# Holding the weight conversions behind block 0's activations, a reciprocal spread by matrix products, and one store per weight chunk

## The chip, the cores and the metric

The kernel runs on one core of a Trainium2 chip. The metric is device time in microseconds (us). Three runs of the kernel before gave 976.02, 977.13 and 977.84 us; their median is 977.13.

## The reference

Three layers follow each other. All inputs are float32, except that the eight-byte weights `w_in` and `w_out` arrive as pairs of 32-bit words, which the kernel has to convert to float32 itself.

1. Linear attention, 8 batches, 8 heads, 576 positions, 64 features: `phi(x)` projects by `w_phi` (64 to 128), subtracts the largest absolute value of the row, and joins `exp(p)` with `exp(-p)`. With `k_p = phi(k)` and `q_p = phi(q)`: `kv = k_p' v`, `z = sum(k_p)`, and the output is `(q_p kv) / (q_p z + 1e-6)`.
2. A dense layer over the 4608 tokens with 512 features: `h = x w_in` (2048 wide), a leaky rectifier with a slope `alpha` for each of the 2048 columns, and a product with `w_out`.
3. A soft mixture of 8 experts with 4 slots each: logits from `phi`, a softmax over all tokens, a two-layer network in each expert, and a softmax over slots for the way back.

## The kernel before

The 4608 tokens are cut into 12 blocks of 384 (`NB`, `BT`); `w_in` is cut into 16 chunks of 128 columns (`NC`). One slot of the program is one product of a block with a chunk: `gemm(n, c)` (L531), 12 matmuls of 128x384 with `x` and `w_in` each split in a high and a low part (`xhi`, `xlo`, `w` in the wring pool). Block n fills slots 16n to 16n+15. Slots below 0 are the opening, in which there is no `gemm` yet. `at(slot, phase, fn)` puts all other work in a slot, before the product ("pre"), beside it ("pe", "pe2") or behind it ("post"). A planner then orders the instructions of each engine ahead of time: it goes by a simulated time line and takes, among the instructions that are ready, the one that stands first in the program. So the order on an engine is fixed when the kernel starts, and an instruction that waits holds up all that stand behind it on its engine. All loads and stores go through one queue, that of SP, in order. A `nosync` dependency between two instructions of one engine fixes only their order in this plan.

The work around the change:

- `conv` (L185) converts a chunk, or two at once, of `w_in` or `w_out`. It loads the words into `raw` (three buffers, L190 to L192), takes the absolute value on ScalarE (ACT, L200) and runs six operations on VectorE (DVE, L201 and L205 to L212). `use_w_in` splits the result: the high part on ACT (L226), the low part on DVE (L227). `behind` (L202) orders the first operations behind others; before, chunks 0 to 2 name key features there, chunk 3 and the pairs from 4 on name nothing. Chunks 0 to 3 sit at slots -30, -26, -22 and -3, the pairs from chunk 4 on at slots 0, 2, 4, ... 10.
- `use_w_out` stores each converted chunk of `w_out` to DRAM in four pieces (L235), and multiplies it with `phi` on TensorE (PE) for the logits. The `w_out` pairs begin at slot 10.
- `k_pair` (L263) makes keys and values of two heads: `project` (L297), `features` (L283: a reduction L285, a subtraction L287, two exponentials L290 and L291), `kv` (L340 to L348), `turn` and `keep` (L362, L369). Pairs 0 to 3 serve batch 0 and so block 0, pairs 4 to 7 batch 1; block 1 needs both. The projected keys lie in the PSUM tile `banks("pk")`, which has one buffer and is shared with the query projections of blocks from 1 on.
- `q_pair` (L389) projects queries, takes the largest absolute value over partitions on GpSimd (POOL, L423), and in `attend` makes `num` and `den` (L444, L449).
- `q_finish` (L461) turns these into `x`: a reciprocal of `den` (L466, L467), a spread of it over partitions, a multiplication, and the split into `xhi` (ACT, L484) and `xlo` (DVE, L485). Block 0 spreads by 16 small matmuls with columns of the identity (`spread`, L488, results in PSUM, L495 multiplies). All other blocks store the reciprocal to DRAM (L470), load it back with every row repeated (`widen`, L475), and multiply (L502). Block 0 divides 1 slot after its reciprocal, block 1 3 slots, the others 6. `xhi` and `xlo` have one buffer each, so block 1's `x` is written only when block 0's last product has read its own.
- `leaky` (L543) takes each product out of PSUM with ACT (L545) and DVE (L546); two PSUM buffers stand for it.

Of the kernel before, what the change touches and what calls it, by code (L numbers as in the profile page):

```python
# [11 lines left out]
I32 = mybir.dt.int32  # L12
U32 = mybir.dt.uint32
AF = mybir.ActivationFunctionType
ALU = mybir.AluOpType
AX = mybir.AxisListType
# [10 lines left out]
BT = 384  # L27
# [34 lines left out]
def attention_prelu_softmoe(ctx: ExitStack, tc, qT, kT, v, wphi, w_in, w_out, alpha, phi, w1, w2, out):  # L62
    nc = tc.nc

    ps_h = ctx.enter_context(tc.tile_pool(name="ps_h", bufs=2, space=PSUM))
# [47 lines left out]
    def bank(name, pool=None):  # L113
        if pool is not None:
            return pool.tile([128, 512], F32, tag={id(ps_h): "h", id(ps_l): "l", id(ps_d): "d"}[id(pool)], name=name)
        taken["a"].append([])
        return ps_a.tile([128, 512], F32, tag="a", name=name)
# [67 lines left out]
    def conv(slot, srcs, uses, behind=None):  # L185
        st = {}
        n = len(srcs)

        def load():
            st["raw"] = prep.tile([128, 2, 1024], I32, tag="raw", name="raw", bufs=3)[:, 0:n]  # L190
            for j in range(n):
                nc.sync.dma_start(st["raw"][:, j], srcs[j])  # L192

        def first():
            pair = st["raw"].rearrange("p c (n t) -> p c n t", t=2)
            st["low"], high = pair[:, :, :, 0].bitcast(U32), pair[:, :, :, 1]
            m = st["m"] = prep.tile([128, 2, 512], F32, tag="m", name="m", bufs=2)[:, 0:n]
            rest = st["rest"] = high.bitcast(F32)
            mu, ru = m.bitcast(U32), rest.bitcast(U32)
            heads = [nc.scalar.activation(m, high.bitcast(F32), AF.Abs)]  # L200
            heads.append(nc.vector.tensor_scalar(out=m, in0=m, scalar1=F64_LEAST, scalar2=F64_MOST, op0=ALU.max, op1=ALU.min))  # L201
            if behind is not None:  # L202
                for ins, other in zip(heads, done_k[behind]):
                    tc.add_manual_dep(ins.ins, other.name, nosync, reason="behind the features of K")
            nc.vector.tensor_scalar(out=mu, in0=mu, scalar1=3, scalar2=0x3FFFFFFF, op0=ALU.logical_shift_left, op1=ALU.bitwise_and)  # L205
            nc.vector.scalar_tensor_tensor(out=mu, in0=high.bitcast(U32), scalar=0xC0000000, in1=mu, op0=ALU.bitwise_and, op1=ALU.bitwise_or)  # L206
            nc.vector.tensor_scalar(out=ru, in0=mu, scalar1=0xFF800000, scalar2=None, op0=ALU.bitwise_and)
            nc.vector.scalar_tensor_tensor(out=rest, in0=st["low"], scalar=2.0 ** -52, in1=rest, op0=ALU.mult, op1=ALU.mult)  # L208

        def second():  # L210
            m = st["m"]
            mark[slot + 1] = nc.vector.tensor_tensor(out=m, in0=m, in1=st["rest"], op=ALU.add).ins  # L212
            for j, use in enumerate(uses):
                use(slot + j, m[:, j])

        at(slot - 2, "pre", load)
        at(slot, "pre", first)
        at(slot + 1, "pre", second)
# [12 lines left out]
    def use_w_out(c):  # L231
        def use(slot, w):
            st = {}
            for i in range(4):
                nc.sync.dma_start(wo32[4 * i + c // 4, 32 * (c % 4):32 * (c % 4) + 32, :], w[32 * i:32 * i + 32])  # L235

            def trans():
                pt = bank("pwt")
                for k in range(KD):
                    nc.tensor.transpose(pt[:, 128 * k:128 * k + 128], w[:, 128 * k:128 * k + 128], ident)  # L240
                st["wT"] = prep.tile([128, 512], F32, tag="wT", name="wT")
                nc.scalar.copy(st["wT"], pt)

            def product():
                pw = bank("pw", ps_l)
                for k in range(KD):
                    nc.tensor.matmul(pw[32 * k:32 * k + 32, 0:128], phi_sb[:, k, :], st["wT"][:, 128 * k:128 * k + 128], start=True, stop=True)
                st["sw"] = prep.tile([128, 128], F32, tag="sw", name="sw")
                nc.scalar.copy(st["sw"], pw[:, 0:128])

            def gather():
                pw = bank("pw2", ps_l)
                nc.tensor.matmul(pw[:, 0:32], st["sw"], tident[:, 0:32], start=True, stop=True)
                nc.vector.tensor_copy(wpr[:, c, :], pw[:, 0:32])

            at(slot + 2, "pe", trans)
            at(slot + 3, "pe", product)
            at(slot + 4, "pe", gather)
        return use
# [3 lines left out]
    def k_pair(slot, i):  # L263
# [18 lines left out]

        def features(src, dst, nt, read):  # L283
            mx = att.tile([128, 4], F32, tag="mx", name="mx", bufs=4)
            nc.vector.tensor_reduce(out=mx[:, 0:nt], in_=src, axis=AX.X, op=ALU.max, apply_absolute_value=True)  # L285
            neg = dst[:, :, 1, :]
            ins = nc.vector.tensor_tensor(out=neg, in0=src, in1=mx[:, 0:nt].unsqueeze(2).to_broadcast([128, nt, F]), op=ALU.subtract).ins  # L287
            if read is not None:
                read.append(ins)
            nc.scalar.activation(dst[:, :, 0, :], neg, AF.Exp)  # L290
            done_k[i] = nc.scalar.activation(neg, neg, AF.Exp, scale=-1.0).ins, ins  # L291
# [169 lines left out]
    def q_finish(slot, n):  # L461
        st = q_st[n]

        def recip():
            rd = sm.tile([128, BT], F32, tag="dT", name="rd")[:, 0:HB]
            nc.vector.tensor_scalar(out=rd, in0=st["den"][:, 0:HB], scalar1=1e-6, scalar2=None, op0=ALU.add)  # L466
            nc.vector.reciprocal(out=rd, in_=rd)  # L467
            st["rd"] = rd
            for j in range(2 if n else 0):
                nc.sync.dma_start(rc_d[n % 2][j].rearrange("p h t -> h p t"), rd[64 * j:64 * j + 64])  # L470

        def widen():
            bc = st["bc"] = xp.tile([128, NP, BT], F32, tag="bc", name="bc")
            for j in range(2):
                nc.sync.dma_start(  # L475
                    bc[64 * j:64 * j + 64], rc_d[n % 2][j, 0:NP].rearrange("p h t -> p (h t)").unsqueeze(0).to_broadcast([64, NP, BT]))

        def scale(p):
            def go():
                if p == 0:  # L480
                    xhi_t[n] = xp.tile([128, KD, BT], F32R, tag="xhi", name="xhi")
                    xlo_t[n] = xp.tile([128, KD, BT], F32R, tag="xlo", name="xlo")
                xs = st["num"][:, p, :]
                nc.scalar.copy(xhi_t[n][:, p, :], xs)  # L484
                nc.vector.tensor_tensor(out=xlo_t[n][:, p, :], in0=xs, in1=xhi_t[n][:, p, :], op=ALU.subtract)  # L485
            return go

        def spread(p):  # L488
            wide = bank("wide", ps_h)
            together([  # L490
                lambda j=j, h=h, sl=slice(64 * j, 64 * j + 64): nc.tensor.matmul(
                    wide[sl, HB * h:HB * h + HB], ident[sl, 64 * j + 32 * h + p:64 * j + 32 * h + p + 1].to_broadcast([64, 64]), st["rd"][sl],
                    start=True, stop=True)
                for h in range(2) for j in (1, 0)])
            nc.vector.tensor_tensor(out=st["num"][:, p, :], in0=wide[:, 0:BT], in1=st["num"][:, p, :], op=ALU.mult)  # L495

        def divide(p):
            def go():
                if n == 0:
                    return spread(p)  # L500
                xs = st["num"][:, p, :]
                ins = nc.vector.tensor_tensor(out=xs, in0=st["bc"][:, p, :], in1=xs, op=ALU.mult).ins  # L502
                tc.add_manual_dep(ins, mark[max(k for k in mark if k <= slot + wait)].name, nosync, reason="behind the load")
            return go

        wait = (1, 3)[n] if n < 2 else 6
        at(slot, "post", recip)
        if n:
            at(slot + 1, "pre", widen)
        for p in range(NP):  # L510
            at(slot + wait, "post", divide(p))
        for p in range(NP):
            at(slot + wait, "post", scale(p))
# [175 lines left out]
    for n in range(NB):  # L689
# [3 lines left out]
            else:  # L693
                q_pair(NC * (n - 1) + 3 * p - 6 - (p > 0) if n > 2 else 12 + 2 * p if n > 1 else (0, 2, 5, 8)[p], n, p)
        q_finish((-22, 12)[n] if n < 2 else NC * (n - 1) + 7, n)
    for c, slot, behind in ((0, -30, 2), (1, -26, 3), (2, -22, 3), (3, -3, None)):
        conv(slot, [w_in[c].bitcast(I32)], [use_w_in], behind)
    for c in range(4, NC, 2):
        conv(c - 4, [w_in[d].bitcast(I32) for d in (c, c + 1)], [use_w_in] * 2)
    for c in range(0, NC, 2):  # L700
        conv(int(10 + 1.2 * c), [w_out[d].bitcast(I32) for d in (c, c + 1)], [use_w_out(d) for d in (c, c + 1)])
    for n in range(NDEF, NB):
# [286 lines left out]
```

## Time and profile before

| what | value |
|---|---|
| three runs, median (lowest to highest) | 977.13 us (976.02 to 977.84) |
| the profiled execution's own time | 975.91 us |
| its span, first to last instruction | 973.9 us |
| its mean granted TensorE clock | 0.987 |
| PE busy with matmuls | 931.4 us, 96% of the span |
| PE weight loads (PEld), which run beside matmuls | 653.7 us, 67% |
| DVE busy | 709.7 us, 73% |
| ACT busy | 410.3 us, 42% |
| POOL busy | 148.4 us, 15% |

Times inside the profile count from the first instruction, and the profiled execution's own time is 2.0 us longer than its span. A busy share is an average over the whole span, in which the opening (the first 70 us) and the later blocks are very different. The granted clock is 1.00 at the full level of 2.4 GHz and 0.50 at 1.2 GHz; a mean between them is a stretch that holds both.

### The profile page before, as it was taken

The numbers are of one execution on the slowest core, as the hardware profiler recorded it, in microseconds if no ns is written. First come the engines' busy times: TensorE is split into PE (matmuls) and PEld (weight loads), VectorE is DVE, ScalarE is ACT, GpSimd is POOL, SyncE is SP. The second block draws the span as 40 slices with busy tenths as digits, with TensorE's granted clock in tenths as the row PEclk, the third lists the DMA queues.
The fourth block names the chain that finished last, engine by engine and source line by source line (L and its number), as shares of the span: only waits on it lengthen the run. The fifth ranks groups of instructions, "written<-read, shape, count | busy, mean of one in ns | idle before, by whom it ended". The sixth has DMA issues, their size and how long they took to land.

```text
span 973.9 us, 19896 instructions
## 1 busy us (share of the span) xinstructions
PE 931.4 (96%) x8210; PEld 653.7 (67%) x8210; DVE 709.7 (73%) x1341; ACT 410.3 (42%) x789; POOL 148.4 (15%) x84
## 2 busy tenths in 40 slices
PE   7978996999999999999999999999999999899997
PEld 4546774677767676676677676776777767787444
DVE  6899996897577587767777677777766767865233
ACT  6655654545445334345345336354343351221113
POOL 5111220301201212122021122111021220000000
PEclk9979998999999999999999999999999999999999
DMA  7346665553131131021121121210111508588999
GB/s 262 116 162 206 204 207 154 176 173 114 54 87 34 31 84 44 23 78 44 35 71 42 33 72 31 70 31 23 46 34 51 178 29 269 172 270 265 329 351 327
DMA packets 75382, 121.34 MB, mean 125 GB/s; under 512 B 7836, under 2 KB 49308, under 8 KB 75292
## 3 DMA queue, kind: packets, MB, share of 16 engines
q1 hardware_dynamic: 75292, 120.07, 39.5%
q8 instruction: 65, 1.06, 0.5%
q14 instruction: 25, 0.20, 0.1%
HBM read 99.03 MB, written 21.00 MB: 123 GB/s over the span
## 4 chain that ended last, share of the span: by engine, by line
PE 79%; DVE 13%; ACT 4%; DMA 2%; issue 1%; SPq 0%; ACTq 0%; DVEq 0%
PE ph L538 39%; PE num L444 6%; PE pkv L340 5%; PE pS L643 4%; PE pl L574 4%; PE den L449 3%; PE pq L411 3%; PE pk L297 2%; PE pso L887 2%; PE pe L867 1%; PE po L923 1%; DVE m L206 1%; DVE m L212 1%; PE pt L362 1%; DVE raw L208 1%
## 5 line engine op out<-in xcount | busy, mean ns | idle before, releaser
L538 PE MATMUL ph<-xhi,w 128*128 128x384 f32 x1536 | 433.4, 351 | 11.5 <-ACT xhi L484 6.1
L538 PEld LDWEIGHTS ph<-xhi,w 128*128 128x128 f32 x1536 | 279.4, 189 | 74.6 <-issue 41.0
L538 PE MATMUL ph<-xlo,w 128*128 128x384 f32 x768 | 257.3, 341 | 0.1
L423 POOL PARTITION_ALL_REDUCE mb<-pj x48 | 141.9, 2957 | 468.4 <-ACT pj L417 374.2
L545 ACT ACTIVATE gT<-ph 128x384 f32<-128x384 f32 x192 | 93.7, 489 | 252.6 <-PE ph L538 248.5
L546 DVE SCALAR_TENSOR_TENSOR gT<-gT,alpha_rest,ph 128x384 f32<-128x384 f32 x192 | 115.7, 603 | 109.2 <-ACT gT L545 108.4
L538 PEld LDWEIGHTS ph<-xlo,w 128*128 128x128 f32 x768 | 144.3, 189 | 11.4 <-issue 8.0
L565 DVE STREAM_TRANSPOSE gb<-gT 128x384 f32<-128x384 f32 x162 | 91.8, 571 | 3.0 <-issue 0.2
L433 ACT ACTIVATE qe<-pj 128x768 f32<-128x768 f32 x90 | 71.8, 838 | 26.7 <-DVE pj L427 18.3
L444 PE MATMUL num<-qe,kv 128*64 128x192 f32 (+1 forms) x488 | 70.0, 412 | 3.6 <-ACT kall L290 2.3
L340 PE MATMUL pkv<-kall 128*64 128x256 f32 x464 | 57.5, 391 | 2.9 <-ACT num L454 1.8
L285 DVE TENSOR_REDUCE mx<-pk 128x4 f32<-128x512 f32 (+1 forms) x80 | 49.5, 623 | 10.4 <-PE pk L297 9.1
L290 ACT ACTIVATE kall<-kall 128x512 f32<-128x512 f32 x60 | 37.5, 627 | 37.6 <-DVE kall L287 37.4
L411 PE MATMUL pq<-qraw,wp 64*128 64x384 f32 x192 | 46.6, 544 | 6.5 <-DMA qraw<-in_qT_dram 3.8
L444 PEld LDWEIGHTS num<-qe,kv 128*64 128x64 f32 x488 | 31.2, 136 | 27.8 <-issue 17.9
L328 DVE TENSOR_TENSOR ks<-ks,kall 128x256 f32<-128x256 f32 x96 | 47.5, 511 | 0.4
L340 PEld LDWEIGHTS pkv<-kall 128*64 128x64 f32 x464 | 31.2, 138 | 23.9 <-issue 5.8
L427 DVE TENSOR_TENSOR pj<-pj,mb 128x768 f32<-128x768 f32 x48 | 44.7, 932 | 2.4 <-POOL mb L423 2.4
L449 PE MATMUL den<-qe,zt 128*32 128x192 f32 x720 | 42.0, 337 | 1.7 <-ACT qe L433 1.7
L287 DVE TENSOR_TENSOR kall<-pk,mx 128x512 f32<-128x512 f32 x60 | 40.9, 681 | 2.4 <-PE pkv L340 1.7
L454 ACT COPY num<-num 128x384 f32<-128x384 f32 x48 | 22.7, 476 | 44.2 <-PE num L444 42.5
L297 PE MATMUL pk<-wp,kall 64*128 64x128 f32 x512 | 38.9, 290 | 2.3 <-DMA kall<-in_kT_dram 1.3
(204 smaller groups left out, 1104.5 us busy)
## 6 DMA issues: line engine op xcount, KB each, us to landing
w<-in_w_dram SPq DMA_DIRECT2D x46, 256.0 KB
kall<-in_v_dram SPq DMA_DIRECT2D x30, 320.0 KB
qraw<-in_qT_dram SPq DMA_DIRECT2D x48, 192.0 KB
out_dram<-os SPq DMA_DIRECT2D x18, 512.0 KB
bc<-rc_d SPq DMA_DIRECT2D x22, 384.0 KB
raw<-in_w_in_dram SPq DMA_DIRECT2D x16, 512.0 KB
raw<-in_w_out_dram SPq DMA_DIRECT2D x16, 512.0 KB
gT_d<-gT SPq DMA_DIRECT2D x32, 192.0 KB
```

Source lines behind the costliest of these rows:

```text
L285: nc.vector.tensor_reduce(out=mx[:, 0:nt], in_=src, axis=AX.X, op=ALU.max, apply_absolute_value=True)
L297: lambda t=t, j=j, sl=slice(64 * j, 64 * j + 64): nc.tensor.matmul(st["pk"][:, j, F * t:F * t + F], st["kraw"][sl, 128 * t:128 * t + 128], ...
L340: return lambda: nc.tensor.matmul(pkv[64 * j:64 * j + 64, 0:256], st["vt"][:, t, 64 * j:64 * j + 64], part.rearrange("p s f -> p (s f)"), ...
L411: lambda j=j, sl=slice(64 * j, 64 * j + 64): nc.tensor.matmul(pq[j][:, 0:BT], wp[sl, F * j:F * j + F], st["qraw"][sl], start=True, stop=True)
L423: nc.gpsimd.partition_all_reduce(mb, pj, 128, bass_isa.ReduceOp.absmax)
L433: nc.scalar.activation(st["e", s], pj, AF.Exp, scale=(1.0, -1.0)[s])
L444: lambda s=s, j=j: nc.tensor.matmul(num[64 * j:64 * j + 64, o:o + w], kvs[:, s, 64 * j:64 * j + 64], st["e", s][:, j, o:o + w], start=(s = ...
L449: lambda s=s, j=j, h=h, zt=kv_t[NP * ((n * BT + h * HB) // S) + p][1]: nc.tensor.matmul(den[64 * j + 32 * h:64 * j + 32 * h + 32, 0:HB], z ...
L538: gemm_last[0] = nc.tensor.matmul(h, (w_in_hi, w_in_lo)[a][c][:, 128 * k:128 * k + 128], (xhi, xlo)[b][:, k, :], start=(i == 0), stop=(i = ...
L545: nc.scalar.activation(gT, h, AF.Relu, scale=-1.0)
L546: ins = nc.vector.scalar_tensor_tensor(out=gT, in0=gT, scalar=alpha_rest[:, c:c + 1], in1=h, op0=ALU.mult, op1=ALU.add).ins
L565: nc.vector.transpose(out=half_of(n, c // 8)[:, c % 8, :], in_=gT)
```

## The change

Three edits, in one step.

1. Chunks 2 and 3 of `w_in` move to slots -19 and -16, and all conversions of `w_in` from chunk 2 on are ordered behind block 0's `x`: their first ACT operation behind the last `xhi` copy, their first DVE operation behind the last `xlo` subtraction (both now kept in `done_k["x", n]`). The feature reductions of key pairs 4 and 5 are ordered behind that `xlo` too.
2. Block 1's reciprocal is spread by 16 matmuls, as block 0's is, into PSUM tiles of the pool that most of the attention uses (`bank(...)` with no pool, two buffers). Its two stores to DRAM, its two loads back and its tile `bc` are gone, and its division stands 1 slot after the reciprocal instead of 3.
3. `use_w_out` stores a chunk with one DMA of 128 rows instead of four of 32.

```diff
-            for i in range(4):
-                nc.sync.dma_start(wo32[4 * i + c // 4, 32 * (c % 4):32 * (c % 4) + 32, :], w[32 * i:32 * i + 32])
+            nc.sync.dma_start(wo32[c // 4::4, 32 * (c % 4):32 * (c % 4) + 32, :], w)
...
-            nc.vector.tensor_reduce(out=mx[:, 0:nt], in_=src, axis=AX.X, op=ALU.max, apply_absolute_value=True)
+            ins = nc.vector.tensor_reduce(out=mx[:, 0:nt], in_=src, axis=AX.X, op=ALU.max, apply_absolute_value=True).ins
+            if 4 <= i < 6:
+                tc.add_manual_dep(ins, done_k["x", 0][1].name, nosync, reason="behind block 0's x")
...
-            for j in range(2 if n else 0):
+            for j in range(2 if n > 1 else 0):
...
-                nc.scalar.copy(xhi_t[n][:, p, :], xs)
-                nc.vector.tensor_tensor(out=xlo_t[n][:, p, :], in0=xs, in1=xhi_t[n][:, p, :], op=ALU.subtract)
+                done_k["x", n] = (
+                    nc.scalar.copy(xhi_t[n][:, p, :], xs).ins,
+                    nc.vector.tensor_tensor(out=xlo_t[n][:, p, :], in0=xs, in1=xhi_t[n][:, p, :], op=ALU.subtract).ins)
...
         def spread(p):
-            wide = bank("wide", ps_h)
+            wide = bank("wide", None if n else ps_h)
+            read = taken["a"][-1:] if n else []
...
-            nc.vector.tensor_tensor(out=st["num"][:, p, :], in0=wide[:, 0:BT], in1=st["num"][:, p, :], op=ALU.mult)
+            ins = nc.vector.tensor_tensor(out=st["num"][:, p, :], in0=wide[:, 0:BT], in1=st["num"][:, p, :], op=ALU.mult).ins
+            for r in read:
+                r.append(ins)
...
-                if n == 0:
+                if n < 2:
                     return spread(p)
...
-        wait = (1, 3)[n] if n < 2 else 6
+        wait = 1 if n < 2 else 6
...
-        if n:
+        if n > 1:
             at(slot + 1, "pre", widen)
...
-    for c, slot, behind in ((0, -30, 2), (1, -26, 3), (2, -22, 3), (3, -3, None)):
+    for c, slot, behind in ((0, -30, 2), (1, -26, 3), (2, -19, ("x", 0)), (3, -16, ("x", 0))):
...
-        conv(c - 4, [w_in[d].bitcast(I32) for d in (c, c + 1)], [use_w_in] * 2)
+        conv(c - 4, [w_in[d].bitcast(I32) for d in (c, c + 1)], [use_w_in] * 2, ("x", 0))
```

## Rows read from the trace of the kernel before

**Rows 1.** The page: busy time and share of the span, instructions, per engine.

```profile
PE 931.4 (96%) x8210; PEld 653.7 (67%) x8210; DVE 709.7 (73%) x1341; ACT 410.3 (42%) x789; POOL 148.4 (15%) x84
```

**Rows 2.** Six stretches: length, busy time of each engine, granted clock, DMA share.

```profile
0.00:37.00 37.00, 30.88 (x337) 18.32 (x339) 23.33 (x55) 24.18 (x44) 12.65 (x16) 1.00 0.60 198
37.00:71.60 34.60, 27.84 (x267) 16.05 (x264) 34.46 (x59) 19.13 (x33) 4.51 (x2) 0.85 0.46 167
71.60:137.10 65.50, 59.42 (x535) 46.89 (x535) 64.46 (x86) 33.99 (x58) 14.95 (x8) 0.97 0.60 198
137.10:170.00 32.90, 23.92 (x192) 16.85 (x191) 25.29 (x44) 17.13 (x34) 3.88 (x3) 0.90 0.57 172
170.00:190.00 20.00, 19.36 (x156) 12.94 (x155) 19.45 (x28) 9.53 (x17) 7.65 (x3) 1.00 0.53 168
190.00:250.00 60.00, 58.93 (x458) 46.53 (x457) 49.57 (x94) 31.13 (x62) 8.69 (x4) 1.00 0.49 143
```

**Rows 3.** Time line of PE, 39 to 67 us: end of block 0's attention, spread, first product.

```profile
39.37 1.43 PE L348 MATMUL pkv<-kp,ones 128*32 128x128 f32 x40
42.37 0.55 PE L362 MATMUL pt<-ident,kvT 128*128 128x128 f32 x3
47.66 0.51 PE L449 MATMUL den<-kall,zt 128*32 128x192 f32 x8
55.96 2.83 PE L491 MATMUL wide<-rd,ident 64*64 64x192 f32 x16 [2.30 <-DVE rd L467]
61.68 1.52 PE L491 MATMUL wide<-rd,ident 64*64 64x192 f32 x16
66.55 0.97 PE L538 MATMUL ph<-xhi,w 128*128 128x384 f32 x4
```

**Rows 4.** Time line of DVE, 42 to 72 us: a conversion's operation, the keep, the reciprocal, `x`.

```profile
42.70 0.68 DVE L212 TENSOR_TENSOR m<-m,raw 128x512 f32<-128x512 f32 x1
43.30 0.42 DVE L207 TENSOR_SCALAR raw<-m 128x512 uint32<-128x512 uint32 x1
44.96 0.42 DVE L369 COPY kv<-pt 128x256 f32<-128x256 f32 x1
51.90 0.35 DVE L466 TENSOR_SCALAR rd<-den 128x192 f32<-128x192 f32 x1
54.57 1.34 DVE L467 RECIPROCAL rd<-rd 128x192 f32<-128x192 f32 x1
59.03 0.54 DVE L495 TENSOR_TENSOR num<-wide,num 128x384 f32<-128x384 f32 x1
71.04 0.55 DVE L485 TENSOR_TENSOR xlo<-num,xhi 128x384 fp32r<-128x384 f32 x1
```

**Rows 5.** Block 1's reciprocal: time lines of DVE, SP's queue and PE, 134 to 156 us.

```profile
135.78 1.35 DVE L467 RECIPROCAL rd<-rd 128x192 f32<-128x192 f32 x1
134.98 5.23 SPq L235 DMA_DIRECT2D wo<-m  x8
141.76 1.19 SPq L470 DMA_DIRECT2D rc_d<-rd  x2
147.04 1.47 SPq L475 DMA_DIRECT2D bc<-rc_d  x2
153.83 0.56 DVE L502 TENSOR_TENSOR num<-bc,num 128x384 f32<-128x384 f32 x1 [6.90 <-DMA bc<-rc_d]
140.17 0.34 PE L538 MATMUL ph<-xhi,w 128*128 128x384 f32 x1
154.99 1.33 PE L538 MATMUL ph<-xhi,w 128*128 128x384 f32 x3 [6.05 <-ACT xhi L484]
```

**Rows 6.** Stretches of 4 us, columns as in rows 2: the clock after both stalls.

```profile
52.00:56.00 4.00, 1.70 (x10) 0.52 (x6) 4.00 (x7) 2.19 (x3) 0.00 (x0) 0.50 0.74 282
152.00:156.00 4.00, 1.01 (x3) 0.82 (x3) 2.17 (x5) 1.57 (x3) 0.00 (x0) 0.71 0.50 164
156.00:160.00 4.00, 4.00 (x19) 2.28 (x18) 4.00 (x9) 1.56 (x4) 0.00 (x0) 0.50 0.28 82
```

**Rows 7.** SP's queue, whole span: one line's issues, least/median/most ns, first and last.

```profile
L235 SPq DMA_DIRECT2D wo<-m x64: 302/423/1200, 127.5 to 239.8; - x64
```

**Rows 8.** The page, DMA issues: tiles, count, size of one issue.

```profile
bc<-rc_d SPq DMA_DIRECT2D x22, 384.0 KB
raw<-in_w_in_dram SPq DMA_DIRECT2D x16, 512.0 KB
```

## The prediction

> **What bounds the kernel now.** I read the page's busy times first. PE is busy 96% of the span [rows 1], so the whole can only lose what PE idles or does at half clock. Then I cut the first 250 us into stretches, since the edits touch nothing behind them [rows 2]. Idle PE is length minus busy: 6.1 us to 37, 6.8 in 37.0 to 71.6, 6.1 in 71.6 to 137.1, 9.0 in 137.1 to 170, 0.6 to 190, 1.1 to 250. Beside it stands DVE: 34.46 of 34.6 and 64.46 of 65.5 us, so from 37 to 137 DVE has no free time, and whatever PE lacks there it lacks because DVE has not yet come to it. In 137.1 to 170 it is the other way: DVE is busy 25.29 of 32.9 us, and both engines wait.
>
> The time lines say for what. First stall: block 0's last attention product ends at 48.2 [rows 3], but its reciprocal begins at 51.9, ends at 55.9, and the last `xlo` ends at 71.6 [rows 4], since each of these steps stands in DVE's order among conversions and key features. PE idles or runs at the 1.2 GHz level meanwhile (clock 0.50 in 52 to 56 with 1.70 of 4 us busy [rows 6]). Second stall: block 1's reciprocal ends at 137.1; SP is then issuing eight stores of `w_out` (134.98, 5.23 us), so the reciprocal's stores go at 141.8, the loads back at 147.0, and the first multiplication runs at 153.8, after DVE has idled 6.90 us. Block 0's last product ended at 140.5, block 1's first starts at 155.0 after 6.05 us of idle PE [rows 5], and the clock is then 0.50 to 160 [rows 6].
>
> **Part by part.** The sum is made against the profiled execution's own 975.9 us; the median of the runs shown is 1.2 us above that.
>
> *The reciprocal of block 1.* Removed: two stores, two loads, and the wait for them. Added: 16 products of 64x192, which block 0's show at 1.52 us at full clock and 2.83 us at half [rows 3]. The four multiplications read PSUM instead of SBUF: 0.54 us against 0.56 [rows 4, 5], so nothing. What can be won is the slack of 137.1 to 170 [rows 2]. On PE: 9.0 us idle, and the half clock, which cost half of the 4.00 us busy in 156 to 160 and half of the 1.01 in 152 to 156 [rows 6], 2.5 together; less 1.5 for the added products, 10.0 us. On DVE the same stretch can shrink only by its idle 32.9 - 25.3 = 7.6 us. Which of the two rules is not shown by the stretch itself: from 170 to 190 PE is busy 19.36 and DVE 19.45 of 20 us, but from 190 to 250 DVE has 10.4 us to spare and PE 1.1 [rows 2], so a DVE that is late can be made good and a PE that is late cannot. I take the middle, 8.8, and keep 7.6 and 10.0. What is late next: `xhi` has one buffer, so block 1's `x` waits for the end of block 0's last product. With the spread, the reciprocal no longer ends last there; that product does, and PE has the key products and `w_out` transposes in between to fill the half microsecond of the copies.
>
> *The hold behind block 0's `x`.* It removes no work; it reorders DVE and ACT. Without conversions in the way, the chain is this. The counts of key pair 3 end at 40.8 and the turn at 42.9 [rows 3]; the keep now starts at once instead of at 44.96 [rows 4], so the 2.0 us it waited go, and `den` ends at 46.1 instead of 48.2. The reciprocal takes 0.35 + 1.34 = 1.7 us: 47.8. Half a microsecond for the first spread product and its latency (an estimate: a quarter of the 1.52 us of all 16): 48.3. Then four multiplications and four subtractions at 0.54 and 0.55 [rows 4], 4.4 us: `x` is whole at 52.7 instead of 71.6, 18.9 us sooner.
>
> But DVE pays for it. Between 37 and 52.7 it may now do only the rest of chunk 1 (five operations of at most 0.68 us, 3.4), two keeps (0.8), the reciprocal (1.7) and `x` (4.4): 10.3 of 15.7 us [rows 4]. The other 5.4 us it idles, where it had 0.1 us idle in the whole stretch [rows 2]. What was done there before is done after 52.7, so DVE reaches its old state of 71.6 about 5.4 us late. Chunks 0 and 1 are enough for PE's first two products, but the third needs chunk 2, and the third needs also that `leaky` of the first has been run, behind the held work in DVE's order. With no slack on DVE until 137 [rows 2], the 5.4 us reappear whole at block 1's reciprocal: 137.1 becomes about 142.5, and block 0's last product ends near 146 instead of 140.5. Block 1's first product then follows within a microsecond or so of it, at 146 to 148 instead of 155.0. The bill is 5.4; its bounds are nothing (if work that DVE does early now need not be done before block 1) and 10.7 (5.4 and one wait for a load, see the last rival). Below nothing is excluded: an order alone cannot make DVE's work less. The half clock of the first stall gives nothing back by itself, since DVE paces that part.
>
> *Behind the hold* stand on ACT the absolute values of the chunks, on DVE the features of key pairs 4 and 5, and through their PSUM tile the first query projections of block 1 on PE. All of these serve block 1, 80 us away, and cost nothing beyond the bill. On SP the load of pair 6/7 now waits for chunk 2's buffer; all later loads queue behind it. About 15 us of held DVE work cover that wait.
>
> *One store for four.* 48 issues of 0.42 us [rows 7] leave SP's queue between 127 and 240. The case where that was in the way, the 5.23 us ahead of the reciprocal's stores [rows 5], is gone through the spread already. What is left is at most the 1.7 us that PE idles from 170 to 250 [rows 2]; the buffer is freed by the last of the four stores as by the one, so it costs nothing. I take nothing.
>
> Sum: -8.8 + 5.4 = -3.4. 975.9 becomes 972.5, and a median of runs 1.2 above it: **973.7 us**.
>
> The Trainium skill speaks against counting PE here: its page "Perfetto Trace Analysis", section "Identifying the Most-Contended Engine", holds that matmul busy time is a poor measure of how near a kernel is to its limit, that weight-load share should be used for TensorE, and that for VectorE the busy share is a fair measure. In 71.6 to 137.1 the weight loads fill 46.89 of 65.5 us beside 59.42 for matmuls and 64.46 for DVE [rows 2], so the trace agrees for that stretch. By that rule DVE's time alone would count, to 190 at least, which is the first rival.
>
> **The rivals.**
>
> 1. DVE alone decides, no change. Only DVE's own idle time counts: 7.6 us won in 137.1 to 170, against 5.4 lost in the hold, or 6.6 if neighbouring operations overlap by 0.08 us as 42.70 + 0.68 against a start at 43.30 shows [rows 4] (15 operations). Net -1.0 to -2.2, so about 975.5. For it: DVE's busy time up to 190 [rows 2]. Against: its 10.4 us of slack right after. Chance 0.19.
> 2. The hold is free. If the planner puts other work into the 5.4 us, or what DVE did early was not needed before block 1, the full PE side counts: -10.0, and -1.7 with the stores: 965.4. For it: PE idles 6.8 us in the first stall. Against: DVE is busy without a break for 100 us. Chance 0.13.
> 3. The spread blocks PE. The products stand in PE's order and wait there for the reciprocal, as block 0's did for 2.30 us [rows 3], and share two PSUM buffers with all the attention. The change would then not do all it says: -3.4 + 2.3, 976.0. Chance 0.06.
> 4. Slower: the conversions starve. Chunks 2 and 3 now hold two of three `raw` buffers through the hold, and SP's queue stands still behind the load of pair 6/7. If the held work does not cover it, DVE waits a whole load: 384 KB took from 148.5 to 153.8, 5.3 us [rows 5], and the pair is two of 512 KB [rows 8]. Then -7.6 + 5.4 + 5.3 = +3.1, 980.2. It decides from the point where DVE waits over 4 us for words between 53 and 100. For it: the deep prefetch is what let DVE run without a break. Against: the 15 us of cover. Chance 0.17.
>
> **How the numbers follow.** My forecast has 0.45, with its own range of 970.5 to 975.1. About 0.2%, 2 us, is what a measurement here can tell from no change. Faster by more: forecast and rival 2, 0.58. Within it: rivals 1 and 3, 0.25. Slower: rival 4, 0.17. The range of 8 in 10 reaches to both far cases, 966.5 to 980.5, and leaves out about half of rival 2 and half of rival 4.
>
> **What would show it.** Hold: the last `xlo` of block 0 near 53, and DVE idle of some 5 us between 37 and 53; if DVE idles under 2 us, rival 2. Bill: block 1's reciprocal ending near 142.5; at 137 or sooner the bill was wrong. Spread: no DVE idle over 2 us around it, no `ph` wait of 6 us, block 1's first product at 146 to 148, clock 1.00 from 150 to 160. Rival 3 would show as a PE wait on `wide` for `rd`. Rival 4 as DVE or ACT idle before L200 and L201 between 53 and 100. The forecast is wrong altogether if PE's idle time after 170 grows by more than it shrank before.

## The result and the profile after

The changed kernel takes 982.75 us (median of 4 runs, 980.80 to 984.18) against 976.58 us for the kernel before in the same session: a ratio of 1.0062 with a 95% interval of 1.0038 to 1.0086. By that ratio it is slower by 6.1 us, where 3.4 us less were forecast. The profiled execution took 982.11 us, its span is 980.2 us. Lines have moved by a few: `spread` is now L494, its multiplication L498, `xhi` L486, `xlo` L487, `gemm` L543, the store L234.

The busy times of the page, to lay beside [rows 1], hardly differ, so the change lies in where the engines wait:

```profile
PE 936.7 (96%) x8242; PEld 656.5 (67%) x8242; DVE 704.4 (72%) x1341; ACT 409.5 (42%) x789; POOL 152.1 (16%) x84
```

The stretches of [rows 2] from 37 us on, same columns:

```profile
37.00:71.60 34.60, 28.50 (x294) 19.41 (x290) 27.66 (x52) 15.25 (x28) 5.89 (x2) 1.00 0.42 146
71.60:137.10 65.50, 58.46 (x527) 42.85 (x528) 65.47 (x90) 40.78 (x69) 20.61 (x10) 0.97 0.56 192
137.10:170.00 32.90, 22.74 (x149) 16.07 (x148) 26.64 (x42) 9.67 (x20) 1.69 (x1) 0.74 0.46 149
170.00:190.00 20.00, 20.00 (x160) 13.55 (x160) 15.55 (x25) 11.52 (x21) 6.45 (x3) 1.00 0.65 207
190.00:250.00 60.00, 58.50 (x473) 46.14 (x468) 50.36 (x90) 32.40 (x63) 7.67 (x5) 1.00 0.46 138
```

In the first two the hold does what it says: DVE is idle for 6.9 of 34.6 us and then without a break, and the clock of the first stall is 1.00 instead of 0.85. The third got worse, though the spread was to empty it: PE is busy 22.74 us instead of 23.92, at a clock of 0.74 instead of 0.90.

The time line of DVE, to lay beside [rows 4] and [rows 5]:

```profile
45.69 0.36 DVE L467 TENSOR_SCALAR rd<-den 128x192 f32<-128x192 f32 x1 [3.05 <-PE den L450]
52.75 1.03 DVE L487 TENSOR_TENSOR xlo<-num,xhi 128x384 fp32r<-128x384 f32 x2
...
135.62 1.34 DVE L468 RECIPROCAL rd<-rd 128x192 f32<-128x192 f32 x1
...
144.18 1.21 DVE L212 TENSOR_TENSOR m<-m,raw 128x1024 f32<-128x1024 f32 x1
...
149.52 0.56 DVE L498 TENSOR_TENSOR num<-wide,num 128x384 f32<-128x384 f32 x1
156.29 0.69 DVE L201 TENSOR_SCALAR m<-m 128x1024 f32<-128x1024 f32 x1 [6.22 <-ACT m L200]
```

Block 0's `x` is whole at 53.8 us (71.6 before). Block 1's reciprocal ends at 137.0, as before. But the first `w_out` pair is converted (L212) only at 145.4, and after one multiplication of block 1 DVE stands still for 6.22 us. PE and ACT in the same place:

```profile
145.44 1.97 PE L239 MATMUL pwt<-ident,m 128*128 128x128 f32 x8 [6.24 <-DVE m L212]
147.34 0.66 PE L246 MATMUL pw<-wT,phi_sb 128*32 128x128 f32 x8
147.92 1.55 PE L494 MATMUL wide<-rd,ident 64*64 64x192 f32 x8
149.40 0.64 PE L252 MATMUL pw<-tident,sw 128*128 128x32 f32 x2
149.96 2.83 PE L494 MATMUL wide<-rd,ident 64*64 64x192 f32 x16
156.71 1.33 PE L543 MATMUL ph<-xhi,w 128*128 128x384 f32 x3 [3.92 <-ACT xhi L486]
```

```profile
155.14 1.12 ACT L200 ACTIVATE m<-raw 128x1024 f32<-128x1024 f32 x1 [6.33 <-DMA wo<-m]
156.16 0.50 ACT L486 CAST xhi<-num 128x384 fp32r<-128x384 f32 x1
```

Two stalls have taken the place of the one of 6.05 us in [rows 5]. PE first waits 6.24 us for the late `w_out` pair, whose transposes stand in its order ahead of the spread. Then ACT, whose next instruction is the absolute value of the third `w_out` pair, waits 6.33 us for a store of `w_out` to free that pair's buffer; `xhi` of block 1 stands behind it, so PE waits another 3.92 us. The clock answers as in [rows 6]:

```profile
152.00:156.00 4.00, 0.79 (x6) 0.17 (x2) 0.00 (x0) 0.86 (x1) 0.00 (x0) 0.50 0.50 156
156.00:160.00 4.00, 3.29 (x17) 1.94 (x19) 3.71 (x7) 1.18 (x3) 0.00 (x0) 0.50 0.60 240
```

SP issued that store at 145.41:

```profile
145.41 1.27 SPq L234 DMA_DIRECT2D wo<-m  x2
146.73 1.48 SPq L192 DMA_DIRECT2D raw<-in_w_out_dram  x2
```

It is two stores of 256 KB, one for each chunk of the pair. The last of the two issues ended at 146.68, and ACT went on at 155.14: 8.5 us. The DMA view of 145.4 to 157 us in 40 slices (busy share of the 16 DMA engines in tenths, and what they moved) shows how:

```profile
DMA  0000131495689999999433322232222496799999
GB/s 0 0 0 0 42 35 7 21 113 85 127 304 346 388 396 353 388 381 403 177 155 155 127 106 78 92 92 71 71 85 106 127 226 198 282 388 388 410 374 396
```

While a load of `raw` runs beside it, the share is 8 or 9 tenths for most of the time and 300 to 400 GB/s move. When that load is nearly through, the share falls to 2 or 3 tenths, what 4 busy engines of 16 would give, and the rate to 71 to 155 GB/s. The single packets in the trace say the same: the pair's 256 packets of 2 KB run from 146.7 to 154.7 us, mostly 4 at a time.

### The profile page after: what moved, and what is told of

It is laid out like the page before. It is cut to its first block, busy times and chain, and to the rows that moved or that the text cites. A ratio compares the mean times of both kernels' runs of the same rounds, so it can differ in the third digit from the quotient of the medians.

```text
span 980.2 us, 19895 instructions
## 1 busy us (share of the span) xinstructions
PE 936.7 (96%) x8242; PEld 656.5 (67%) x8242; DVE 704.4 (72%) x1341; ACT 409.5 (42%) x789; POOL 152.1 (16%) x84
## 4 chain that ended last, share of the span: by engine, by line
PE 83%; DVE 8%; DMA 4%; ACT 3%; issue 1%; SPq 0%; DVEq 0%; ACTq 0%
PE ph L543 39%; PE pkv L341 7%; PE num L445 7%; PE pS L648 4%; PE pl L579 4%; PE den L450 4%; PE pq L412 3%; PE pk L298 3%; PE pso L892 2%; PE pe L872 1%; PE po L928 1%; PE pt L363 1%; DVE gT L551 1%; DMA wo<-m 1%; PE idle L108 1%
## 5 line engine op out<-in xcount | busy, mean ns | idle before, releaser
L543 PE MATMUL ph<-xhi,w 128*128 128x384 f32 x1536 | 430.8, 350 | 13.0 <-DVE gT L551 3.9
L543 PEld LDWEIGHTS ph<-xhi,w 128*128 128x128 f32 x1536 | 278.5, 188 | 77.7 <-issue 39.7
L543 PE MATMUL ph<-xlo,w 128*128 128x384 f32 x768 | 257.0, 341 | 0.1
L424 POOL PARTITION_ALL_REDUCE mb<-pj x48 | 146.0, 3042 | 486.7 <-ACT pj L418 403.4
L543 PEld LDWEIGHTS ph<-xlo,w 128*128 128x128 f32 x768 | 144.0, 188 | 10.2 <-issue 7.5
L418 ACT COPY pj<-pq 128x768 f32<-128x768 f32 x44 | 35.0, 795 | 14.1 <-PE pq L412 14.1
```

The costliest lines, as they stand in the source:

```text
L424: nc.gpsimd.partition_all_reduce(mb, pj, 128, bass_isa.ReduceOp.absmax)
L543: gemm_last[0] = nc.tensor.matmul(h, (w_in_hi, w_in_lo)[a][c][:, 128 * k:128 * k + 128], (xhi, xlo)[b][:, k, :], start=(i == 0), stop=(i = ...
```

## The experiments

Ratios are to the kernel before, run on the same chip in the same session, with 95% intervals; 0.001 is 1.0 us. "Theory A" is that the spread stands behind other work on PE and ACT, B that the hold's bill is the loss, C that the store is slow to land. The recorded texts call A' the part of A that lies in PE's order, B' the bill that has to be paid somewhere, C' a store that moves on 4 DMA engines.

**The three edits, alone and in pairs.** Each kernel is the one before with the lines of one or two of the edits shown above (here shortened).

```diff
 hold_only:
+(2, -19, ("x", 0)), (3, -16, ("x", 0))):  and  [use_w_in] * 2, ("x", 0))  and  if 4 <= i < 6: ...
 spread_only:
+if n < 2: return spread(p)  and  wait = 1 if n < 2 else 6
 store_only:
+nc.sync.dma_start(wo32[c // 4::4, 32 * (c % 4):32 * (c % 4) + 32, :], w)
```

> The kernel before with the hold alone (chunks 2 and 3 moved, conversions of w_in and key pairs 4 and 5 behind block 0's x); block 1's reciprocal still goes through DRAM and each w_out chunk is stored in four pieces. Theory A (the loss comes from block 1's spread, which stands on PE behind w_out transposes and on ACT behind an absolute value that waits for a w_out store): the hold by itself costs what VectorE idles in it, 5 to 7 us, less what block 1's wait on DRAM hides: 978 to 983. Theory B (the hold's bill is the whole loss and the spread brings nothing): 982 to 984. Theory C (the single store is slower to land and is the loss): 975 to 978, like before.

Measured: 1.0006 [0.9993, 1.0019]. PE's wait of 6.05 us for `xhi` [rows 5] is gone and another of the same length stands there (engine, tile and line, waited for: us in total, times, longest):

```profile
PE pwt L240 <- DVE m L212: 6.2, 1, 6.2
```

The busy times of its two stretches:

```profile
0.00:137.10 137.10, 119.13 (x1130) 80.95 (x1132) 114.85 (x191) 78.76 (x137) 38.38 (x25) 0.99 0.53 180
137.10:170.00 32.90, 26.21 (x186) 20.81 (x185) 32.08 (x51) 14.55 (x30) 2.95 (x2) 0.90 0.61 185
```

DVE has done 114.85 us of work by 137.1, 7.4 less than before (122.25, the third figure behind the length in the first three rows of [rows 2], added up). It does 32.08 us in the next stretch, where it did 25.29. DVE's wait for `bc` is 0.31 us here, 6.90 before. So a hold alone pays its bill out of time that DVE idled anyway. The median, 977.15 us, lies in C's range, below those of A and B.

> The kernel before with block 1's reciprocal spread by products, without the hold and with four stores per chunk. Theory A: the first w_out pair is converted by 134 as before, so its transposes do not hold up PE, and block 1's x comes some 7 us earlier: 968 to 973. Theory B: 975 to 978. Theory C: 967 to 973.

Measured: 0.9925 [0.9909, 0.9941], 7.3 us faster. That lies in the ranges of A and C; B, by which the spread brings nothing, fell. The second stall is gone, and by 137.1 DVE is as far as before:

```profile
0.00:137.10 137.10, 118.93 (x1113) 81.74 (x1113) 121.95 (x195) 77.24 (x133) 32.03 (x24) 0.96 0.54 186
137.10:170.00 32.90, 32.38 (x272) 22.18 (x269) 31.06 (x51) 20.13 (x38) 5.24 (x5) 1.00 0.58 191
```

> The kernel before with one store per w_out chunk and nothing else. Theory A and B: SyncE issues block 1's reciprocal 3 to 4 us earlier, so 972 to 977. Theory C: 980 to 984.

Measured: 1.0069 [1.0045, 1.0093], 6.7 us slower by one line, as C has it; A and B expected no loss. SP's queue and DVE where block 1's reciprocal goes through DRAM:

```profile
139.31 3.41 SPq L469 DMA_DIRECT2D rc_d<-rd  x2
...
150.24 1.55 SPq L474 DMA_DIRECT2D bc<-rc_d  x2
```

```profile
157.31 1.96 DVE L501 TENSOR_TENSOR num<-bc,num 128x384 f32<-128x384 f32 x4 [14.14 <-DMA bc<-rc_d]
```

The loads back are issued 7.5 us after the stores, 4.1 before (147.04 against 142.95), and DVE waits 14.14 us for them instead of 6.90 [rows 5].

> The changed kernel without the hold (chunks 2 and 3 back at slots -22 and -3). Theory A: w_out's conversions are on time, so neither transposes nor stores hold up block 1's x: 968 to 973. Theory B: 975 to 978. Theory C: 980 or more.

Measured: 0.9935 [0.9919, 0.9950]. C fell here, A's range holds: with the spread and no hold the slow store costs next to nothing. The `w_out` pairs are converted in time, SP issues the first pair's store at 129.74, and ACT waits only 1.2 us for its buffer.

> The changed kernel with four stores for each chunk of w_out again. Theory C' (the single store, whose destination has 4 as its outermost size, moves on about 4 of the 16 DMA engines, and everything behind it waits): without it the absolute value of the third w_out pair no longer waits 6 us for a store and block 1's first product starts at 148 to 151; 969 to 975. Theory A (the hold alone makes the w_out transposes late for the spread, whatever the store): 978 to 983.

Measured: 1.0012 [0.9996, 1.0027]. With four stores the other two edits together still gain nothing: A's range holds, and the 969 to 975 us of C' missed, though ACT's wait for a store is down to 1.7 us. PE's time line has the same wait of 6.2 us for the late `w_out` pair:

```profile
148.86 1.97 PE L240 MATMUL pwt<-ident,m 128*128 128x128 f32 x8 [6.21 <-DVE m L212]
```

**One store on all the engines.** Chunk c goes to 128 plain rows of DRAM instead of 4 groups of 32, and the later reload puts the order right with four loads.

```diff
-nc.sync.dma_start(wo32[c // 4::4, 32 * (c % 4):32 * (c % 4) + 32, :], w)
+nc.sync.dma_start(wo32[c], w)
...
+i, q = divmod(key[1], 4)
+for j in range(4):
+    nc.sync.dma_start(t[32 * j:32 * j + 32], wo32[4 * q + j, 32 * i:32 * i + 32, :])
```

> The changed kernel with still one store per chunk of w_out, but into a destination of 128 plain rows (the regrouping moved to the late reloads, in four parts each). Theory C': the store uses all DMA engines and lands in 2 to 3 us instead of 8 to 9; 968 to 975, as without the edit. If the size of one store, not its outermost dimension, is the trouble: 980 to 984, as changed. Theory A: 978 to 983.

Measured: the changed kernel with it takes 0.9984 [0.9972, 0.9997], so the form of one store is worth 0.0078, or 7.6 us. At 975.67 us it is just above the range of C' and below the others. ACT no longer waits for a store:

```profile
150.30 1.17 ACT L200 ACTIVATE m<-raw 128x1024 f32<-128x1024 f32 x1
151.71 0.51 ACT L486 CAST xhi<-num 128x384 fp32r<-128x384 f32 x1 [0.24 <-DVE num L498]
```

The first pair's 256 packets of 2 KB now run from 147.8 to 149.5 us, mostly 15 to 17 at a time: 1.7 us instead of 8.0. The DMA view of the same 145.4 to 157 us has single slices at 3 tenths and no stretch of them:

```profile
DMA  9300000069999999998799899999973695789866
GB/s 381 106 0 0 0 0 0 0 233 367 374 396 318 191 367 367 353 438 240 297 353 438 360 403 374 389 381 304 388 184 127 169 297 170 268 311 381 311 268 283
```

The other stall is still there, as in the kernel with four stores:

```profile
147.04 1.97 PE L239 MATMUL pwt<-ident,m 128*128 128x128 f32 x8 [6.24 <-DVE m L212]
```

> The kernel before with one store per chunk into 128 plain rows, nothing else. Theory C': block 1's reciprocal is issued 3 to 4 us earlier and is not behind slow stores: 971 to 976. If one large store by itself is the trouble: 980 to 985, as the single store in the changed shape gave (982.8).

Measured: the kernel before with this store alone takes 0.9978 [0.9962, 0.9995]. One store for four is a small gain where it moves on all engines.

> No hold: the kernel before with the spread by products and the single store on all 16 engines. If the two gains add (spread 0.9925, wide store 0.9978): 0.990. If the store only shortened the wait that the spread removes anyway: 0.992 to 0.993, the same as the spread alone.

Measured: 0.9925 [0.9909, 0.9942], the same as the spread alone. The store's small gain lay in the stall that the spread removes.

**Where the hold's bill lands.** Three tries to take the `w_out` pairs out of the way.

```diff
 after_held4 (the changed kernel):
-[use_w_out(d) for d in (c, c + 1)])
+[use_w_out(d) for d in (c, c + 1)], ("x", 1) if c >= 4 else None)
 wide_later_wout (after_wide):
-conv(int(10 + 1.2 * c), ...
+conv(int(12 + c), ...
 wide_later_wout_held: the same, and
+... , ("x", 1) if c >= 2 else None)
 spread_and_wide_later_wout: int(12 + c) in spread_and_wide_store
```

> The changed kernel with the conversions of w_out from its third pair on held behind block 1's x, on ScalarE and VectorE. Theory C' and A agree that xhi then does not stand behind the absolute value that waits for a store: block 1's first product at about 151 instead of 156.7, the 6.2 us wait of PE on the transposes stays; 975 to 979.

Measured: 1.0036 [1.0022, 1.0051], 2.5 us better than the changed kernel; 975 to 979 us were expected, 980.59 came out, and block 1's first product starts at 157.9. The absolute value that waits for the store now stands behind `xhi`, and the wait of 3.92 us is gone; the one for the late pair is not:

```profile
150.01 1.97 PE L239 MATMUL pwt<-ident,m 128*128 128x128 f32 x8 [6.24 <-DVE m L212]
```

> The changed kernel with the store of all 16 engines, and the w_out pairs moved from slots int(10 + 1.2 c) to slots 12 + c, so that the first w_out transposes stand behind the spread of block 1 in PE's order. Theory A' (what the hold costs is PE's order: transposes that wait for a late conversion stand ahead of the spread): the wait of 6.2 us of `pwt` ahead of `wide` is gone, `wide` starts near 142 instead of 149, ratio to before 0.990 to 0.995. Rival B' (the 5.4 us of DVE idle in the hold must be paid wherever): the ratio stays near that of the version with the earlier pairs, 0.997 to 1.000, and PE waits as long for something else between 137 and 170.

Measured: 1.0011 [0.9995, 1.0026]. Theory A' fell, and the ratio is just above the range of B' too. The transposes stand behind the spread now and the first two spreads run at once, but then PE waits for DVE, which has no idle time from 137 to 163 and reaches the first multiplication at 147.62 (PE, then DVE):

```profile
142.58 1.52 PE L494 MATMUL wide<-rd,ident 64*64 64x192 f32 x16
148.22 1.55 PE L494 MATMUL wide<-rd,ident 64*64 64x192 f32 x8 [4.12 <-DVE num L498]
```

```profile
147.62 0.55 DVE L498 TENSOR_TENSOR num<-wide,num 128x384 f32<-128x384 f32 x1
```

> As the version with later w_out pairs, and all w_out pairs but the first ordered behind block 1's x on DVE and ACT. Theory A' with DVE's interleaving as its second half (block 1's x was spread out between conversions from 149.5 to 164.9): x of block 1 whole 5 us sooner, ratio 0.988 to 0.993. Rival B': 0.997 to 1.000; a third way: the held conversions come late for their own consumers, 0.996 or more with a new wait of `pwt` behind block 1's first products.

Measured: 0.9960 [0.9946, 0.9974], 5 us better than without the second hold. It is above the range that A' gave, but below what B' gave: with the debt put behind block 1's `x`, the last `xlo` of block 1 ends at 150.6 instead of 156.7. Still, PE waits 4.25 us for the first multiplication.

```profile
149.38 1.22 DVE L487 TENSOR_TENSOR xlo<-num,xhi 128x384 fp32r<-128x384 f32 x2
```

> No hold, spread, wide store, w_out pairs at slots 12 + c. It shows what the later slots do by themselves. Theory A': without the hold the conversions are on time, so there is no wait to remove and the ratio is that of the version with earlier pairs within 0.002. If the later slots alone gain 0.003 or more, the gain of the held version with later slots says nothing of the hold.

Measured: 0.9945 [0.9927, 0.9964]. The later slots alone gain nothing, so the 5 us above belong to the held kernel. Laid side by side, the two kernels differ by 0.0015, though the hold of block 0 leaves DVE 7.1 us behind by 137.1 (the third figure behind the length; this kernel, then wide_later_wout_held):

```profile
0.00:137.10 137.10, 117.51 (x1124) 80.63 (x1126) 122.29 (x197) 76.95 (x133) 32.26 (x25) 0.96 0.56 191
0.00:137.10 137.10, 117.37 (x1149) 79.80 (x1150) 115.18 (x193) 78.53 (x139) 37.38 (x26) 0.99 0.53 180
```

Where the work that DVE owes stands behind block 1's `x`, then, the debt costs about 1.5 us (up to 4 by the intervals) instead of 7. The second hold without the first was not run, so it is not excluded that part of this is a gain of its own.

**Is it DVE's time?** Theory D: the hold leaves DVE behind, and the only idle time that could pay is the one that the spread also takes. Two kernels hold only half; two leave out the operations L205 and L206 of four conversions, 7.6 us by their durations, so that DVE gets the lost time back.

```diff
 hold_late_only (hold_and_spread):
-(2, -19, ("x", 0)), (3, -16, ("x", 0))):
+(2, -22, 3), (3, -3, None)):
 hold_23_only (hold_and_spread):
-[use_w_in] * 2, ("x", 0))
+[use_w_in] * 2)
-if 4 <= i < 6:
+if False:
 hold_spread_light, spread_light (hold_and_spread, spread_only):
+if not 4 <= slot < 12 or uses[0] is not use_w_in:
     nc.vector.tensor_scalar(out=mu, ...)
     nc.vector.scalar_tensor_tensor(out=mu, ...)
```

> Hold and spread with four stores, but chunks 2 and 3 as before the change (slots -22 and -3, not behind block 0's x): only the pairs from chunk 4 on and the features of key pairs 4 and 5 are held. Theory D: the ratio exceeds the spread's 0.9925 by what DVE's busy time up to 137.1 lacks against the spread alone (121.96 us), a thousandth for each us, whatever that is; since chunk 2 and 3 fill the gap, some 2 to 4 us lacking, ratio 0.995 to 0.997. Rival O: 1.000 or more, since the orders around block 1 are as under the whole hold.

Measured: 0.9945 [0.9924, 0.9967].

> Hold and spread with four stores, but only chunks 2 and 3 held behind block 0's x; the pairs from 4 on and the features of key pairs 4 and 5 free. Theory D: the free work fills DVE's gap, under 3 us lacking up to 137.1, ratio 0.993 to 0.996. Rival O: 0.998 or more.

Measured: 0.9969 [0.9952, 0.9986]. Both are below rival O's bound; the range given for D was missed from below by the first (0.995 to 0.997) and from above by this one (0.993 to 0.996). The stretch to 137.1 of hold_late_only, hold_23_only and hold_and_spread, in this order, then of spread_and_wide_store and after_wide:

```profile
0.00:137.10 137.10, 115.39 (x1132) 81.53 (x1136) 121.03 (x200) 77.08 (x135) 30.05 (x24) 0.99 0.55 184
```

```profile
0.00:137.10 137.10, 119.83 (x1172) 81.94 (x1174) 116.83 (x196) 80.87 (x141) 34.09 (x27) 0.99 0.53 183
```

```profile
0.00:137.10 137.10, 118.82 (x1128) 80.53 (x1128) 113.98 (x191) 78.23 (x136) 38.70 (x25) 0.99 0.53 180
```

```profile
0.00:137.10 137.10, 118.59 (x1112) 81.72 (x1112) 121.03 (x195) 77.14 (x133) 32.11 (x24) 0.96 0.56 191
0.00:137.10 137.10, 117.31 (x1148) 79.81 (x1148) 115.99 (x193) 79.96 (x140) 38.38 (x25) 1.00 0.52 180
```

| held | DVE busy by 137.1 | lacking against the same kernel without a hold | ratio above that kernel's 0.9925 |
|---|---|---|---|
| pairs from chunk 4 on, key pairs 4 and 5 | 121.03 us | 0.9 us | 0.0020 |
| chunks 2 and 3 | 116.83 us | 5.1 us | 0.0044 |
| all, four stores | 113.98 us | 8.0 us | 0.0087 |
| all, one store of 128 rows | 115.99 us | 5.0 us | 0.0059 |

In these four, one lost microsecond of DVE costs about one of the whole, within intervals of 0.0013 to 0.0022 on each side. It is no general rate, since wide_later_wout_held lacks 7.1 us and loses 1.5. My guess of how much each half would lose was wrong for both. It is chunks 2 and 3, not the pairs, that leave DVE without work in the hold.

> Hold and spread, four stores, but of four pairs of w_in (chunks 8 to 15) the operations L205 and L206 are left out of the conversion, so the weights are wrong and DVE has 4 x (0.68 + 1.21) = 7.6 us less to do between 72 and 137. Theory D (the hold's cost is the 6 to 8 us that DVE is behind at 137): ratio 0.992 to 0.995. Rival O (the cost is the order that the planner makes under the hold): 0.998 or more. Either way it is read against the next kernel, with the same operations left out and no hold.

Measured: 0.9955 [0.9938, 0.9972]. Giving DVE 7.6 us back takes 5.6 us off hold_and_spread, a little less than D's range, 0.992 to 0.995, has it.

> The spread alone, no hold, four stores, with the same operations left out as in the kernel before it in this call (7.6 us less on DVE). Where PE has no idle time left after 137, DVE's time is worth only what PE idles before it: Theory D: 0.986 to 0.992, and the hold then costs less than 3 us between these two, where it cost 8.5 between the full ones. Rival O: the hold still costs 6 us or more between them.

Measured: 0.9970 [0.9956, 0.9984], so the hold costs nothing between these two; by 137.1 the held one has done more on DVE (115.23 against 111.45 us), so it carries no debt against the other. But D's number for this kernel was wrong: less work on DVE made the spread alone slower, not faster. In 71.6 to 137.1 DVE does 9.8 us less and PE no more (first row; spread_only has 60.29 for PE, 65.47 for DVE); what DVE waits for there is mostly PE's products, through ACT (second row):

```profile
71.60:137.10 65.50, 60.52 (x529) 48.17 (x525) 55.67 (x80) 35.11 (x59) 18.35 (x7) 0.97 0.69 232
```

```profile
DVE gT L550 <- ACT gT L549: 6.4, 4, 3.8
```

Without the hold, then, time given to DVE alone bought nothing up to 137. Why this kernel is 4.4 us slower than spread_only stays open. The planner orders each kernel anew, and this pair shows that such an order can move the time by as much as half of the largest cost in the table above; D rests on four kernels that agree and is not proven by them.

The fastest version is the spread by itself: 968.43 us, with four stores or with one on all engines.

## Why the prediction was wrong

Two chains of kernels give the three terms. The first adds one edit at a time, as the sum did: spread_only, hold_and_spread, the changed kernel. The second has one store of 128 rows in its first two kernels, spread_and_wide_store and after_wide, and its last step changes the form of that store alone.

| term of the sum | forecast | measured, four stores first | measured, 128 rows first |
|---|---|---|---|
| reciprocal spread by products | -8.8 us | -7.3 us (1 to 0.9925) | -7.3 us (1 to 0.9925, with that store) |
| hold behind block 0's `x` | +5.4 us | +8.5 us (to 1.0012) | +5.8 us (to 0.9984) |
| the store in 4 groups | 0 | +4.9 us (to 1.0062) | +7.6 us (to 1.0062) |
| sum | -3.4 us | +6.1 us | +6.1 us |

The chains share the same total differently because the hold is not the same in both: by 137.1 DVE lacks 8.0 us with four stores and 5.0 with 128 rows, and the changed kernel (116.53 us busy) is as far as after_wide (115.99). So 7.6 us is the cleaner price of the store's form, and 4.9 us is what the edit added to the kernel with the other two. In either chain the store is the term furthest from its forecast, and it alone turns a gain or a draw into a loss.

**The step that failed is the store**: "the buffer is freed by the last of the four stores as by the one, so it costs nothing. I take nothing." I priced the issue on SP's queue [rows 7] and never asked how fast the one transfer moves. Its destination, `wo32[c // 4::4, ...]`, has 4 groups of 32 rows, and the trace shows 4 of its packets at a time, the pair landing 8.5 us after its issue. Writing the same bytes to 128 plain rows removed ACT's wait and 7.6 us. The Trainium skill has the rule that I should have read: its page "DMA: Bandwidth & Descriptors", section "Why a DMA increments its semaphore by 16 and not by 1", says that the number of engines is the largest number up to 16 that divides the slowest dimension above 1 on both sides, here 4. The trace agrees: 4 packets at a time and a share of 2 to 3 tenths. The size of the loss is not the store's own duration. Against four stores it costs 6.7 us alone, where DVE waits longer for `bc`, 1.0 us with the spread, and 4.9 us with spread and hold, where ACT waits. Taking ACT's wait away (after_held4) gave back 2.5 us of the changed kernel's loss, so how the rest comes about is not shown; in that kernel DVE had also done less by 137.1 (113.64 us).

**The hold** was right in its first half: `x` whole at 53.8 us (52.7 forecast), DVE idle 6.9 us in the stretch. Its bill, 5.4 us, came to 5.8 beside the store of 128 rows, but to 8.5 beside four stores, the kernel that the sum passed through; its place was wrong. I looked for it at block 1's reciprocal (142.5 forecast, 137.0 measured, which the prediction had named as the sign that the bill was wrong; 140.4 in hold_and_spread, where part of it did fall there); block 0's last product ended at 138.1, not at 146. The planner runs first what stands first in the program, so, as I read it, the debt of the changed kernel went to the work that stands last: the first `w_out` pair, whose stores begin at 127.5 in [rows 7] and at 145.4 after, 18 us later for about 5 us of debt (116.53 us of DVE work by 137.1 against 121.41 in spread_and_store). There it found PE, since I had also written that "PE has the key products and `w_out` transposes in between to fill": these transposes were themselves what was late. Moving them showed the debt again, as a wait for DVE's multiplication (wide_later_wout); putting the owed conversions behind block 1's `x` as well took most of it away (wide_later_wout_held).

**The spread** was worth 7.3 us, near the bound of DVE's idle time, 7.6. Its interval, 5.8 to 8.9 us, does not exclude the middle of 8.8 that I took, but does exclude the 10.0 of PE. Alone it did all that was forecast: from 137.1 to 170 no wait of PE over 0.4 us, clock 1.00, and block 1's first product at 146.9.

**The rivals.** With the store in 128 rows the time is that of rival 1, DVE alone decides: -1.0 to -2.2 us forecast, -1.6 us measured (after_wide). With four stores, as its sum had them, it is +1.2 us (hold_and_spread), so part of that agreement is luck. Rival 2, a free hold, is refuted beside the spread as the change stands, but true without it (hold_only): the same idle time can pay for a debt or be cut out, once. Its condition, that what DVE did early was not needed before block 1, was nearly met by wide_later_wout_held, where the hold costs 1.5 us. Rival 3 expected the spread to wait for the reciprocal; in the changed kernel it waited behind transposes instead. Rival 4 had the direction by the wrong mechanism: DVE is busy 65.47 of 65.5 us from 71.6 to 137.1, so nothing starved for loads.

## What to carry to other kernels

Before merging transfers, look at how many engines each form moves on, not only at how often it is issued: stores of 256 KB in 4 groups made the kernel 7.6 us slower than the same stores in 128 rows. A hold that idles an engine with no slack is a debt. Here it fell on the last work in that engine's order, so look there for who waits, and see whether the owed work can stand behind the critical chain: that took 5 us off (wide_later_wout_held). And when two edits are priced on the same idle time, price them together: hold and spread gained 0 and 7.3 us alone, and at most 1.6 together.

## What was not expected of the hardware

Two large stores ran beside free DMA engines, 4 packets at a time, and took 8.0 us for 512 KB, while the same bytes in another layout moved 15 to 17 packets at a time in 1.7 us. SP's queue hardly shows the difference: a pair is issued in 1.27 us in the one form and 0.80 in the other. It is seen in the DMA view, and in the engine that waits for the buffer.
